# Channel mixing over token groups of 512, 512, 512 and 256, with every large tile at a multiple of 128 bytes

## The chip, the cores and the metric

The kernel runs on one core of one Trainium2 chip. TensorE (PE) multiplies matrices, VectorE (DVE) and ScalarE (ACT) do elementwise work and can read PSUM, GpSimd (POOL) does elementwise work in SBUF and issues some DMAs, SyncE (SP) issues most DMAs. The metric is the device time of the whole program in microseconds. Three timed runs of the kernel before gave 1157.68, 1158.13 and 1159.16 us; the median is 1158.13 us.

## The reference

Four batches of 448 tokens, 768 channels (12 heads of 64). Three stages follow each other:

```python
scores = scale * np.matmul(q, k.transpose(0, 1, 3, 2)) - np.log(S)
x = np.matmul(1.0 / (1.0 + np.exp(-scores)), v)      # stage 1, then heads side by side

h = x.transpose(0, 2, 1) @ U @ V                     # stage 2
u = x + h.transpose(0, 2, 1)
x = u + np.maximum(u @ w_ch1, 0.0) @ w_ch2           # channel mixing: 768 -> 3072 -> 768

theta = x @ w_theta                                  # stage 3
y = einsum(w_tok_r, x * cos(theta)) + einsum(w_tok_i, x * sin(theta))
u = x + y
out = u + np.maximum(u @ w_ch, 0.0)
```

The channel mixing does not couple tokens: it can be cut over the 4 x 448 = 1792 tokens at any place. The inputs `moe_w_ch1` and the others arrive as 64-bit floats and are turned into 32-bit ones inside the kernel.

## The kernel before

The running value `X` lies in SBUF as [128 channels of a block, 6 blocks, 1792 tokens], float32. To keep float32 accuracy with the one-pass matmul type fp32r, every operand is split into a high part and a low part (`uh`/`ul`, `gh`/`gl`, and two halves of each weight tile `w`), and each product is three matmuls: high x high, high x low, low x high.

The channel mixing is a loop over 12 blocks `i` of 256 hidden channels, and inside it over `b`, the four batches of 448 tokens. `ch1(i, b)` (lines 696 to 713) makes the hidden block: 2 x 6 x 3 = 36 matmuls of 128x128 weights against 448 moving columns into the PSUM tile `g`; then ACT takes the rectified value rounded to fp32r (`gh`, L709), and DVE the rest (`gl`, L710). `ch2(i, b)` (lines 715 to 729) multiplies back: 36 matmuls into three PSUM tiles `y` (two of them exist), and after each of them DVE adds the tile to `X` (L728). PE's order is `ch1` of a block, then `ch2` of the block before: 12 x 4 x 72 = 3456 matmuls in all, lines L702 to L704 and L724 to L726.

The order is written by hand (`manual_schedule`). Conversions of the next weights are jobs of a few steps, `size` on ACT, `bits`, `top`, `word` on DVE, then the split on ACT and POOL. The table `units` puts the steps at places `tick(i, b, t)`: t = 0 before `ch1`, t = 1 before `ch2`, t = 2 to 4 after its three additions. Each engine runs its own instructions in that order.

In the first block of all, `i` = 0, some of stage 2 is still going on. `split_u(b)` makes `uh` on ACT (L109) and `ul` on POOL (L112) or DVE (L118) from `X`. `U2(3)` (L495, L499, tile `hl`) adds the low-rank term of batch 3 to `X`; it runs between the pieces of `ch2(0, 0)`, and the splits of batch 2 stand behind it in the same hook, those of batch 3 one block later.

SBUF places: pools pad each tile to 32 bytes. `bias_s` and `half_pi` take 32 bytes each before `X`, so that in the built program `X` starts at byte 16576, 64 past a multiple of 128; with `warm` behind it, every other large tile starts 96 past one. All strides inside these tiles (1792, 3072, 512 bytes) are multiples of 128, so that every moving operand of an fp32r matmul starts 96 past a multiple of 128.

Of the kernel before, what the change touches and what calls it, by code (L numbers as in the profile page):

```python
# [19 lines left out]
def f(t):  # L20
    return t.bitcast(F32)
# [3 lines left out]
def tile_kernel(  # L25
# [20 lines left out]
    P = 128  # L46
# [40 lines left out]

    bias_s = cpool.tile([P, 1], F32, name="bias_s")
    half_pi = cpool.tile([P, 1], F32, name="half_pi")
    X = cpool.tile([P, NK, NT], F32, name="X")  # L90

    ctx.enter_context(tc.manual_schedule())
# [208 lines left out]
    ap2, ap2_st = pool("ap2")  # L301
    ident = ap2.tile([P, P], F32, name="ident")
    ps_a, ps_a_st = pool("ps_a", "left", PSUM)
# [268 lines left out]

    nc.vector.memset(bias_s, NEG_LOG_S)
    nc.vector.memset(half_pi, math.pi / 2)
    warm = cpool.tile([P, 1], F32, name="warm")
    load_qk(0)
# [22 lines left out]

    def split_u(b, p, d0, d1, *los):  # L600
        if d0 == 0:
            uh_t[b] = p.tile([P, NK, S], F32R, name=f"uh{b}")
            ul_t[b] = p.tile([P, NK, S], F32R, name=f"ul{b}")
# [88 lines left out]

    def ch1(i, b, js=range(FB)):
        if js[0] == 0:
            g_t[i, b] = ps_g.tile([P, FB, 512], F32, tag="g", name=f"g_{i}_{b}", bufs=2)
        ps = g_t[i, b]
        for j in js:
            wh, wl = w1_t[i, j][:, 0], w1_t[i, j][:, 1]
            for kk in range(NK):
                o = ps[:, j, :S]  # L700
                sl = slice(kk * P, (kk + 1) * P)
                nc.tensor.matmul(o, wh[:, sl], uh_t[b][:, kk, :], start=kk == 0, stop=False)  # L702
                nc.tensor.matmul(o, wh[:, sl], ul_t[b][:, kk, :], start=False, stop=False)  # L703
                nc.tensor.matmul(o, wl[:, sl], uh_t[b][:, kk, :], start=False, stop=kk == NK - 1)  # L704
        if js[-1] != FB - 1:
            return
        h = gpool.tile([P, FB, S], F32R, tag="gh", name=f"gh_{i}_{b}", bufs=2)
        l = gpool.tile([P, FB, S], F32R, tag="gl", name=f"gl_{i}_{b}", bufs=2)
# [6 lines left out]
    def ch2(i, b, after):  # L715
        gh, gl = g_t.pop((i, b))
        for e2 in range(NK // 2):
            ps = ps_y.tile([P, 2, 512], F32, tag="y", name=f"y_{i}_{b}_{e2}", bufs=2)
            for e in range(2):
                o = ps[:, e, :S]  # L720
# [20 lines left out]
    split_u(1, u[1][0], 0, NK, lo_pool, lo_dve)  # L741
    ch1(0, 0)
    ch1(0, 1, (0,))
# [3 lines left out]
    hi_act(vll, f(vl[:, (B - 1) % 2]))  # L747
    ch1(0, 1, (1,))
    ap_st.close()
    ps_a_st.close()  # L750

    u23, u23_st = pool("u23")
    ps_y, ps_y_st = pool("ps_y", "left", PSUM)
    def turn_x(b, d, t):
        nc.vector.transpose(out=t, in_=X[:, d, b * S:(b + 1) * S])
        nc.gpsimd.dma_start(out=x_d[d * P:(d + 1) * P, b * S:(b + 1) * S], in_=t)

    def hook(i, b):
# [361 lines left out]
```

## Time and profile before

| | |
|---|---|
| median of three runs | 1158.13 us |
| span of the profiled execution, first to last instruction | 1155.6 us |
| median less that span | 2.5 us |
| PE busy | 1144.3 us, 99% |
| DVE, ACT, POOL busy | 58%, 31%, 18% |
| channel mixing, first to last matmul | 162.9 to 869.8 us |

The profile records the start of each matmul. Its end is modelled, and a recorded duration (366 ns) is longer than the distance to the next start, since matmuls are pipelined; so a busy PE says only that work is queued, and the distance between starts says how fast it goes. PEld is the load of the 128x128 weights for the next matmul, which lies beside the matmul that runs.

### The profile page before, as it was taken

The numbers are of one execution on the slowest core, as the hardware profiler recorded it, in microseconds if no ns is written. First come the engines' busy times: TensorE is split into PE (matmuls) and PEld (weight loads), VectorE is DVE, ScalarE is ACT, GpSimd is POOL, SyncE is SP. The second block draws the span as 40 slices with busy tenths as digits, with TensorE's granted clock in tenths as the row PEclk, the third lists the DMA queues.
The fourth block names the chain that finished last, engine by engine and source line by source line (L and its number), as shares of the span: only waits on it lengthen the run. The fifth ranks groups of instructions, "written<-read, shape, count | busy, mean of one in ns | idle before, by whom it ended". The sixth has DMA issues, their size and how long they took to land.

```text
span 1155.6 us, 15709 instructions
## 1 busy us (share of the span) xinstructions
PE 1144.3 (99%) x6336; PEld 994.2 (86%) x6336; DVE 667.5 (58%) x831; ACT 358.0 (31%) x465; POOL 205.5 (18%) x172
## 2 busy tenths in 40 slices
PE   8999999999999999999999999999999999999998
PEld 5444468999999999999999999999999899999997
DVE  4787873445555555566566656656466643832443
ACT  6777863121212222222222222222014432730110
POOL 4120013210211111111221222111122321420000
PEclk9999999999999999999999999999999999999999
DMA  9898820113232423242414142413248410320444
GB/s 148 163 170 174 161 73 1 56 55 98 67 107 74 123 54 120 66 130 58 148 58 154 65 146 70 144 68 120 73 145 264 68 28 14 73 118 1 64 63 66
DMA packets 222568, 111.20 MB, mean 96 GB/s; under 512 B 188800, under 2 KB 212224, under 8 KB 222368
## 3 DMA queue, kind: packets, MB, share of 16 engines
q1 hardware_dynamic: 193856, 92.60, 31.6%
q0 software_dynamic: 4160, 14.21, 4.1%
q10 hardware_dynamic: 24480, 3.39, 2.0%
q8 instruction: 50, 0.82, 0.3%
q14 instruction: 22, 0.18, 0.1%
HBM read 86.51 MB, written 23.66 MB: 95 GB/s over the span
## 4 chain that ended last, share of the span: by engine, by line
PE 92%; DVE 3%; DMA 2%; ACT 1%; issue 1%; SPq 1%; ACTq 0%; DVEq 0%
PE g L702 10%; PE y L724 10%; PE y L725 10%; PE g L704 10%; PE g L703 10%; PE y L726 10%; PE av L439 4%; PE sc L413 3%; PE y L961 3%; PE y L959 3%; PE y L960 3%; PE wc L1084 2%; PE wc L1082 2%; PE wc L1083 2%; PE th L851 2%; PE th L847 2%
## 5 line engine op out<-in xcount | busy, mean ns | idle before, releaser
L728 DVE TENSOR_TENSOR X<-y,X 128x896 f32<-128x896 f32 x144 | 157.0, 1090 | 105.9 <-PE y L726 104.3
L702 PE MATMUL g<-uh,w 128*128 128x448 f32 x576 | 210.7, 366 | 0.0
L724 PE MATMUL y<-gh,w 128*128 128x448 f32 x576 | 210.6, 366 | 0.0
L704 PE MATMUL g<-uh,w 128*128 128x448 f32 x576 | 210.4, 365 | 0.0
L725 PE MATMUL y<-gl,w 128*128 128x448 f32 x576 | 210.4, 365 | 0.0
L726 PE MATMUL y<-gh,w 128*128 128x448 f32 x576 | 210.4, 365 | 0.0
L703 PE MATMUL g<-ul,w 128*128 128x448 f32 x576 | 210.4, 365 | 0.0
L709 ACT ACTIVATE gh<-g 128x896 fp32r<-128x896 f32 x48 | 44.1, 919 | 377.6 <-PE g L704 377.6
L710 DVE SCALAR_TENSOR_TENSOR gl<-g,gh 128x896 fp32r<-128x896 f32 x48 | 52.4, 1092 | 179.5 <-ACT gh L709 179.5
L112 POOL TENSOR_TENSOR w<-ca_w,w 128x768 fp32r<-128x768 f32 x42 | 77.9, 1854 | 423.2 <-ACT w L109 423.2
L702 PEld LDWEIGHTS g<-uh,w 128*128 128x128 f32 x576 | 108.2, 188 | 9.8 <-ACT uh L109 0.7
L724 PEld LDWEIGHTS y<-gh,w 128*128 128x128 f32 x576 | 108.2, 188 | 9.1 <-issue 0.6
L704 PEld LDWEIGHTS g<-uh,w 128*128 128x128 f32 x576 | 108.2, 188 | 8.6
L726 PEld LDWEIGHTS y<-gh,w 128*128 128x128 f32 x576 | 108.2, 188 | 8.5
L725 PEld LDWEIGHTS y<-gl,w 128*128 128x128 f32 x576 | 108.2, 188 | 8.5
L703 PEld LDWEIGHTS g<-ul,w 128*128 128x128 f32 x576 | 108.2, 188 | 8.5
L390 ACT ACTIVATE A<-sc,bias_s 128x896 f32<-128x896 f32 x72 | 69.9, 1006 | 7.5 <-PE sc L413 7.1
L156 DVE SCALAR_TENSOR_TENSOR ca_w<-ca_w,ws_w 128x768 uint32<-128x768 uint32 x48 | 60.0, 1251 | 3.8
L439 PE MATMUL av<-A,v 128*64 128x448 f32 x288 | 62.1, 552 | 0.0
L961 PE MATMUL y<-tok,zl 128*128 128x448 f32 x168 | 61.5, 366 | 0.3 <-DVE zl L118 0.3
L959 PE MATMUL y<-tok,zh 128*128 128x448 f32 x168 | 61.6, 367 | 0.2 <-ACT zh L109 0.2
L960 PE MATMUL y<-tok,zh 128*128 128x448 f32 x168 | 61.4, 366 | 0.0
(145 smaller groups left out, 1629.0 us busy)
## 6 DMA issues: line engine op xcount, KB each, us to landing
ws_w<-in_moe_w_ch_dram SPq DMA_DIRECT2D x40, 768.0 KB, 4.5
ws_w<-in_moe_w_ch_dram POOLq DMA_DIRECT2D x8, 768.0 KB, 5.5
x_d<-stg POOLq DMA_DIRECT2D x24, 224.0 KB, 2.5
k<-in_k_dram SPq DMA_DIRECT2D x90, 56.0 KB, 3.7
xn<-x_d SPq DMA_DIRECT2D x52, 96.0 KB, 3.3
q<-in_q_dram SPq DMA_DIRECT2D x89, 56.0 KB, 3.2
ws_th<-in_moe_w_theta_dram SPq DMA_DIRECT2D x6, 768.0 KB, 4.3
th_d<-sp_th SPq DMA_DIRECT2D x6, 768.0 KB, 4.0
```

What stands on the lines that cost most here:

```text
L112: nc.gpsimd.tensor_sub(o, a, b)
L439: nc.tensor.matmul(ps[h * D:(h + 1) * D, :S], v_t[p // 2][:, 2 * (p % 2) + h, c, :], A_t[p, c][:, h, :], start=c == 0 and p % 2 == 0, stop ...
L702: nc.tensor.matmul(o, wh[:, sl], uh_t[b][:, kk, :], start=kk == 0, stop=False)
L703: nc.tensor.matmul(o, wh[:, sl], ul_t[b][:, kk, :], start=False, stop=False)
L704: nc.tensor.matmul(o, wl[:, sl], uh_t[b][:, kk, :], start=False, stop=kk == NK - 1)
L724: nc.tensor.matmul(o, wh[:, sl], gh[:, j, :], start=j == 0, stop=False)
L725: nc.tensor.matmul(o, wh[:, sl], gl[:, j, :], start=False, stop=False)
L726: nc.tensor.matmul(o, wl[:, sl], gh[:, j, :], start=False, stop=j == FB - 1)
L728: nc.vector.tensor_add(x, ps[:, :, :S], x)
L959: nc.tensor.matmul(o, zh[:, sl], tok_h[:, i, :], start=first and n == 0, stop=False)
L960: nc.tensor.matmul(o, zh[:, sl], tok_l[:, i, :], start=False, stop=False)
L961: nc.tensor.matmul(o, zl[:, sl], tok_h[:, i, :], start=False, stop=last and n == len(slots) - 1)
```

## The change

The loop over batches in the channel mixing becomes a loop over `GRP`, four groups of 512, 512, 512 and 256 tokens. The number of blocks, of matmuls and of elementwise instructions stays; a matmul has 512 or 256 moving columns in place of 448. Tiles of `uh`, `ul`, `gh`, `gl`, `stg` get the new widths, and the pool of `uh`/`ul` for groups 2 and 3 becomes two pools. The small tiles go elsewhere or are 128 bytes wide, one tile of 96 bytes is put on the right side, and the scratch for software DMA descriptors is 8192 bytes per partition in place of 16384. In the built program every tile above 1 KB, `X` among them, now starts at a multiple of 128 bytes; this holds for the tiles of stages 1 and 3 too, whose widths stay. `gl` (the rectified low part) is emitted behind the first addition of the `ch2` that follows, in place of before it.

```diff
+    GB = 512
+    GRP = [(c, min(c + GB, NT)) for c in range(0, NT, GB)]
+    NG = len(GRP)
...
-    bias_s = cpool.tile([P, 1], F32, name="bias_s")
-    half_pi = cpool.tile([P, 1], F32, name="half_pi")
     X = cpool.tile([P, NK, NT], F32, name="X")
+
+    edge = ctx.enter_context(tc.tile_pool(name="edge", bufs=1, side="right"))
+    edge.tile([P, 24], F32, name="edge")
...
-    ident = ap2.tile([P, P], F32, name="ident")
+    ident = X[:, 0, :P]
+    bias_s, warm = (ap1.tile([P, R], F32, name=name)[:, :1] for name in ("bias_s", "warm"))
...
-    def split_u(b, p, d0, d1, *los):
+    def split_u(g, p, d0, d1, *los):
+        c0, c1 = GRP[g]
...
-            x = X[:, d, b * S:(b + 1) * S]
-            hi_act(uh_t[b][:, d], x)
-            los[d % len(los)](ul_t[b][:, d], x, uh_t[b][:, d])
+            x = X[:, d, c0:c1]
+            hi_act(uh_t[g][:, d], x)
+            los[d % len(los)](ul_t[g][:, d], x, uh_t[g][:, d])
...
-                o = ps[:, j, :S]
+                o = ps[:, j]
                 sl = slice(kk * P, (kk + 1) * P)
-                nc.tensor.matmul(o, wh[:, sl], uh_t[b][:, kk, :], start=kk == 0, stop=False)
+                nc.tensor.matmul(o, wh[:, sl], uh_t[g][:, kk, :], start=kk == 0, stop=False)
...
-        nc.scalar.activation(h, ps[:, :, :S], AF.Relu)
-        nc.vector.scalar_tensor_tensor(
-            out=l, in0=ps[:, :, :S], scalar=0.0, in1=f(h), op0=ALU.max, op1=ALU.subtract
-        )
-        g_t[i, b] = (h, l)
+        nc.scalar.activation(h, ps, AF.Relu)
+        g_t[i, g] = (h, l)
+
+        def low():
+            nc.vector.scalar_tensor_tensor(out=l, in0=ps, scalar=0.0, in1=f(h), op0=ALU.max, op1=ALU.subtract)
+        return low
...
-            x = X[:, 2 * e2:2 * e2 + 2, b * S:(b + 1) * S]
-            nc.vector.tensor_add(x, ps[:, :, :S], x)
+            x = X[:, 2 * e2:2 * e2 + 2, c0:c1]
+            nc.vector.tensor_add(x, ps, x)
+            if e2 == 0 and low is not None:
+                low()
             after(e2)
...
             if i == 0 and b in (1, 2):
-                split_u(b + 1, u23, 2 * e2, 2 * e2 + 2, lo_pool)
+                split_u(b + 1, u[b + 1][0], 2 * e2, 2 * e2 + 2, lo_pool)
...
-        for b in range(B):
+        for b in range(NG):
             tick(i, b, 0)
+            low = None
             if (i, b) not in ((0, 0), (0, 1)):
-                ch1(i, b)
+                low = ch1(i, b)
...
-    nc = _bacc.Bacc("TRN2", target_bir_lowering=False, num_devices=1)
+    nc = _bacc.Bacc("TRN2", target_bir_lowering=False, num_devices=1, dynamic_dma_scratch_size=8192)
```

DVE's rows in the iterations (0, 2) to (1, 0). The names are tiles with their block or group numbers: `gl` the low part, `y` the product back, `ws_w` and `ca_w` a weight in conversion. Before:

```order
L710 SCALAR_TENSOR_TENSOR gl_2_2406<-g_2_2368,gh_2_2405 128x896
L728 TENSOR_TENSOR X<-y_1_0_2409,X 128x2x448
L728 TENSOR_TENSOR X<-y_1_1_2429,X 128x2x448
L728 TENSOR_TENSOR X<-y_1_2_2447,X 128x2x448
L146 TENSOR_SCALAR ws_w_1_1_1742<-ws_w_1_1_1742 128x768
L150 SCALAR_TENSOR_TENSOR ws_w_1_1_1742<-ca_w_1_1_2467,ws_w_1_1_1742 128x768
L156 SCALAR_TENSOR_TENSOR ca_w_1_1_2467<-ca_w_1_1_2467,ws_w_1_1_1742 128x768
L710 SCALAR_TENSOR_TENSOR gl_3_2510<-g_3_2472,gh_3_2509 128x896
L728 TENSOR_TENSOR X<-y_2_0_2516,X 128x2x448
```

The same stretch of the changed kernel:

```order
L735 TENSOR_TENSOR X<-y_1_0_2412,X 128x2x512
L718 SCALAR_TENSOR_TENSOR gl_2_2410<-g_2_2372,gh_2_2409 128x1024
L735 TENSOR_TENSOR X<-y_1_1_2433,X 128x2x512
L735 TENSOR_TENSOR X<-y_1_2_2451,X 128x2x512
L150 TENSOR_SCALAR ws_w_1_1_1743<-ws_w_1_1_1743 128x768
L154 SCALAR_TENSOR_TENSOR ws_w_1_1_1743<-ca_w_1_1_2471,ws_w_1_1_1743 128x768
L160 SCALAR_TENSOR_TENSOR ca_w_1_1_2471<-ca_w_1_1_2471,ws_w_1_1_1743 128x768
L735 TENSOR_TENSOR X<-y_2_0_2519,X 128x2x512
L718 SCALAR_TENSOR_TENSOR gl_3_2514<-g_3_2476,gh_3_2513 128x2x256
```

`gl` of a block has moved from before the first addition to behind it, and the widths are 1024 and 2 x 256 in place of 896.

PE's rows at the end of `ch2(0, 0)`, where the last piece of `U2(3)` (`hl`) stands ahead of `ch1(0, 2)` (`g_2`). Before:

```order
L726 MATMUL y_0_2_2340<-gh_0_2173,w_0_1_1704 128x448
L495 MATMUL hl_2354<-vhl,pc_2253 128x448 x2
L499 MATMUL hl_2354<-vll,pc_2253 128x448 x2
L702 MATMUL g_2_2368<-uh_2310,w_0_0_1026 128x448
L703 MATMUL g_2_2368<-ul_2311,w_0_0_1026 128x448
```

The same place of the changed kernel:

```order
L733 MATMUL y_0_2_2341<-gh_0_2174,w_0_1_1705 128x512
L500 MATMUL hl_2355<-vhl,pc_2254 128x448 x2
L504 MATMUL hl_2355<-vll,pc_2254 128x448 x2
L707 MATMUL g_2_2372<-uh_2311,w_0_0_1027 128x512
L708 MATMUL g_2_2372<-ul_2312,w_0_0_1027 128x512
```

Nothing has moved here, but group 2 is tokens 1024 to 1535 and holds 192 tokens of batch 3 (from token 1344); its splits `uh`, `ul` now need the result of `hl`, pair of channel blocks by pair.

## Rows read from the trace of the kernel before

**Rows 1.** The page: span, engines' busy time, granted clock in 40 slices.
```profile
span 1155.6 us, 15709 instructions
...
PE 1144.3 (99%) x6336; PEld 994.2 (86%) x6336; DVE 667.5 (58%) x831; ACT 358.0 (31%) x465; POOL 205.5 (18%) x172
...
PEclk9999999999999999999999999999999999999999
```

**Rows 2.** Waits: who waited for whom, us in total, times, longest.
```profile
PE warm L596 <- POOL ident masks.py:199: 3.4, 1, 3.4
PE sc L413 <- DVE kl L118: 0.5, 1, 0.5
...
DVE gl L710 <- ACT gh L709: 179.5, 48, 7.3
```

**Rows 3.** Stretch of channel mixing: us, busy and (x) by engine, clock, DMA.
```profile
191.20:869.60 678.40, 678.40 (x3349) 628.82 (x3348) 391.89 (x410) 141.43 (x176) 120.50 (x79) 1.00 0.29 94
```

**Rows 4.** Timeline of PE, ends of channel mixing: start, us, engine, line.
```profile
191.17 0.47 PE L702 MATMUL g<-uh,w 128*128 128x448 f32 x1
...
869.80 0.34 PE L847 MATMUL th<-th_r,xh 128*128 128x384 f32 x1
```

**Rows 5.** Timeline of PE in the projection, 12 matmuls apart, 384 columns.
```profile
1000.60 0.33 PE L847 MATMUL th<-th_r,xh 128*128 128x384 f32 x1
...
1002.68 0.33 PE L847 MATMUL th<-th_r,xh 128*128 128x384 f32 x1
```

**Rows 6.** Timeline of PE in the token mixing, 18 matmuls apart, 448 columns.
```profile
1011.08 0.37 PE L961 MATMUL y<-tok,zl 128*128 128x448 f32 x1
...
1014.80 0.36 PE L961 MATMUL y<-tok,zl 128*128 128x448 f32 x1
```

**Rows 7.** Plain float32 transposes on PE: timeline, then durations min/median/max.
```profile
1015.00 0.82 PE L874 MATMUL xn<-ident_r,X 128*128 128x128 f32 x6
...
L874 PE MATMUL xn<-ident_r,X x6: 270/272/273, 1015.0 to 1015.5; 128*128 128x128 f32 x6
```

**Rows 8.** Timeline of PEld and PE, scores after a pause.
```profile
92.57 0.19 PEld L413 LDWEIGHTS sc<-qh,kh 64*128 64x128 f32 x2 [0.70 <-issue]
92.68 0.19 PEld L413 LDWEIGHTS sc<-ql,kh 64*128 64x128 f32 x2
...
92.88 0.36 PE L413 MATMUL sc<-ql,kh 64*128 64x448 f32 x2
```

**Rows 9.** Timeline: the last matmul of a tile, and the instruction that waited for it.
```profile
402.66 0.36 PE L704 MATMUL g<-uh,w 128*128 128x448 f32 x1
...
403.06 0.92 ACT L709 ACTIVATE gh<-g 128x896 fp32r<-128x896 f32 x1 [10.06 <-PE g L704]
...
1149.82 0.36 PE L1084 MATMUL wcl<-uh,wc_r 128*128 128x448 f32 x1
1150.22 0.62 DVE L1049 SCALAR_TENSOR_TENSOR X<-wcl,X 128x448 f32<-128x448 f32 x1 [2.34 <-PE wcl L1084]
```

**Rows 10.** Groups of instructions by shape: busy us, mean ns, idle before.
```profile
L728 DVE TENSOR_TENSOR X<-y,X 128x896 f32<-128x896 f32 x144 | 157.0, 1090 | 105.9 <-PE y L726 104.3 <-POOL ul L112 1.3
L960 PE MATMUL y<-tok,zh 128*128 128x448 f32 x168 | 61.4, 366 | 0.0
L710 DVE SCALAR_TENSOR_TENSOR gl<-g,gh 128x896 fp32r<-128x896 f32 x48 | 52.4, 1092 | 179.5 <-ACT gh L709 179.5
L848 PE MATMUL th<-th_r,xh 128*128 128x384 f32 x168 | 56.1, 334 | 0.0
L1083 PE MATMUL wc<-ul,wc_r 128*128 128x448 f32 x132 | 48.2, 365 | 0.0
```

**Rows 11.** Timeline around 181 to 192 us: splits of batch 2, addition of `hl`.
```profile
181.34 2.91 ACT L109 ACTIVATE uh<-X 128x448 fp32r<-128x448 f32 x6
...
181.99 6.71 POOL L112 TENSOR_TENSOR ul<-X,uh 128x448 fp32r<-128x448 f32 x6 [12.95 <-ACT uh L109]
...
191.28 1.09 DVE L503 TENSOR_TENSOR X<-hl,X 128x896 f32<-128x896 f32 x1
```

More of the change, by code (lines that the diff above doesn't have):

```diff
@@ L573, in tile_kernel @@
     nc.vector.memset(bias_s, NEG_LOG_S)
-    nc.vector.memset(half_pi, math.pi / 2)
-    warm = cpool.tile([P, 1], F32, name="warm")
     load_qk(0)
@@ L598, in tile_kernel @@
     uh_t, ul_t, g_t = {}, {}, {}
-    def split_u(b, p, d0, d1, *los):
+    def split_u(g, p, d0, d1, *los):
+        c0, c1 = GRP[g]
         if d0 == 0:
-            uh_t[b] = p.tile([P, NK, S], F32R, name=f"uh{b}")
-            ul_t[b] = p.tile([P, NK, S], F32R, name=f"ul{b}")
+            uh_t[g] = p.tile([P, NK, c1 - c0], F32R, name=f"uh{g}")
+            ul_t[g] = p.tile([P, NK, c1 - c0], F32R, name=f"ul{g}")
         for d in range(d0, d1):
-            x = X[:, d, b * S:(b + 1) * S]
-            hi_act(uh_t[b][:, d], x)
-            los[d % len(los)](ul_t[b][:, d], x, uh_t[b][:, d])
+            x = X[:, d, c0:c1]
+            hi_act(uh_t[g][:, d], x)
+            los[d % len(los)](ul_t[g][:, d], x, uh_t[g][:, d])
     warm_up(26)
@@ L691, in tile_kernel, with ch1 @@
     ps_g, ps_g_st = pool("ps_g", "right", PSUM)
-    def ch1(i, b, js=range(FB)):
+    def ch1(i, g, js=range(FB)):
+        w = GRP[g][1] - GRP[g][0]
         if js[0] == 0:
-            g_t[i, b] = ps_g.tile([P, FB, 512], F32, tag="g", name=f"g_{i}_{b}", bufs=2)
-        ps = g_t[i, b]
+            g_t[i, g] = ps_g.tile([P, FB, GB], F32, tag="g", name=f"g_{i}_{g}", bufs=2)
+        ps = g_t[i, g][:, :, :w]
         for j in js:
@@ L699, in ch1, with ch2 @@
             for kk in range(NK):
-                o = ps[:, j, :S]
+                o = ps[:, j]
                 sl = slice(kk * P, (kk + 1) * P)
-                nc.tensor.matmul(o, wh[:, sl], uh_t[b][:, kk, :], start=kk == 0, stop=False)
-                nc.tensor.matmul(o, wh[:, sl], ul_t[b][:, kk, :], start=False, stop=False)
-                nc.tensor.matmul(o, wl[:, sl], uh_t[b][:, kk, :], start=False, stop=kk == NK - 1)
+                nc.tensor.matmul(o, wh[:, sl], uh_t[g][:, kk, :], start=kk == 0, stop=False)
+                nc.tensor.matmul(o, wh[:, sl], ul_t[g][:, kk, :], start=False, stop=False)
+                nc.tensor.matmul(o, wl[:, sl], uh_t[g][:, kk, :], start=False, stop=kk == NK - 1)
         if js[-1] != FB - 1:
             return
-        h = gpool.tile([P, FB, S], F32R, tag="gh", name=f"gh_{i}_{b}", bufs=2)
-        l = gpool.tile([P, FB, S], F32R, tag="gl", name=f"gl_{i}_{b}", bufs=2)
-        nc.scalar.activation(h, ps[:, :, :S], AF.Relu)
-        nc.vector.scalar_tensor_tensor(
-            out=l, in0=ps[:, :, :S], scalar=0.0, in1=f(h), op0=ALU.max, op1=ALU.subtract
-        )
-        g_t[i, b] = (h, l)
-    def ch2(i, b, after):
-        gh, gl = g_t.pop((i, b))
+        h = gpool.tile([P, FB, GB], F32R, tag="gh", name=f"gh_{i}_{g}", bufs=2)[:, :, :w]
+        l = gpool.tile([P, FB, GB], F32R, tag="gl", name=f"gl_{i}_{g}", bufs=2)[:, :, :w]
+        nc.scalar.activation(h, ps, AF.Relu)
[3 more added lines that the diff above has]
+        return low
+    def ch2(i, g, after, low):
+        c0, c1 = GRP[g]
+        gh, gl = g_t.pop((i, g))
         for e2 in range(NK // 2):
-            ps = ps_y.tile([P, 2, 512], F32, tag="y", name=f"y_{i}_{b}_{e2}", bufs=2)
+            ps = ps_y.tile([P, 2, GB], F32, tag="y", name=f"y_{i}_{g}_{e2}", bufs=2)[:, :, :c1 - c0]
             for e in range(2):
-                o = ps[:, e, :S]
+                o = ps[:, e]
                 sl = slice((2 * e2 + e) * P, (2 * e2 + e + 1) * P)
@@ L741, in tile_kernel @@
     split_u(1, u[1][0], 0, NK, lo_pool, lo_dve)
-    ch1(0, 0)
+    ch1(0, 0)()
     ch1(0, 1, (0,))
@@ L747, in tile_kernel, with turn_x @@
     hi_act(vll, f(vl[:, (B - 1) % 2]))
-    ch1(0, 1, (1,))
+    ch1(0, 1, (1,))()
     ap_st.close()
     ps_a_st.close()
-    u23, u23_st = pool("u23")
+    u.append(pool("u2"))
     ps_y, ps_y_st = pool("ps_y", "left", PSUM)
-    def turn_x(b, d, t):
-        nc.vector.transpose(out=t, in_=X[:, d, b * S:(b + 1) * S])
-        nc.gpsimd.dma_start(out=x_d[d * P:(d + 1) * P, b * S:(b + 1) * S], in_=t)
+    def turn_x(g, d, t):
+        c0, c1 = GRP[g]
+        nc.vector.transpose(out=t[:, :c1 - c0], in_=X[:, d, c0:c1])
+        nc.gpsimd.dma_start(out=x_d[d * P:(d + 1) * P, c0:c1], in_=t[:, :c1 - c0])
     def hook(i, b):
         def after(e2):
-            if i == L and 0 < b < B:
+            if i == L and 0 < b < NG:
                 for d in (2 * e2, 2 * e2 + 1):
-                    turn_x(b - 1, d, late["stg"].tile([P, S], F32, tag="stg", name=f"stg_{b}_{d}", bufs=4))
+                    turn_x(b - 1, d, late["stg"].tile([P, GB], F32, tag="stg", name=f"stg_{b}_{d}", bufs=4))
             if (i, b) == (0, 1):
@@ L803, in tile_kernel @@
                 th_t[0] = load_kept("th0", "w1")
-            if i == L and b == B - 1:
+            if i == L and b == NG - 1:
                 th_t[2] = load_kept("th2", "w1")
@@ L810, in tile_kernel @@
             if prev is not None:
-                ch2(*prev, hook(i, b))
+                ch2(*prev, hook(i, b), low)
             prev = (i, b)
@@ L814, in tile_kernel @@
                 uv_st.close()
+                u.append(pool("u3"))
                 late["sp"], sp_st = pool("sp")
-    ch2(*prev, hook(NB - 1, B))
+    ch2(*prev, hook(NB - 1, NG), None)
     th_t[4] = load_kept("th4", "w2")
@@ L821, in tile_kernel @@
     stg_st.close()
-    u23_st.close()
+    u[3][1].close()
+    u[2][1].close()
     gpool_st.close()
@@ L834, in tile_kernel @@
     ctx.enter_context(st)
+    half_pi = zp.tile([P, R], F32, name="half_pi")[:, :1]
+    nc.vector.memset(half_pi, math.pi / 2)
     T_t, z_t, pj_t = {}, {}, {}
@@ L990, in tile_kernel @@
     for d in range(NK):
-        t = zp.tile([P, 2, HN], F32, tag="zh", name=f"stg_{B}_{d}", bufs=12).rearrange("p a n -> p (a n)")[:, :S]
-        turn_x(B - 1, d, t)
+        t = zp.tile([P, 2, HN], F32, tag="zh", name=f"stg_{NG}_{d}", bufs=12).rearrange("p a n -> p (a n)")
+        turn_x(NG - 1, d, t)
     project(0, th_t, "th", 0, 4)
```

## The prediction

> **What bounds the kernel now.** I read the page first: PE is busy for 1144.3 of 1155.6 us and its clock is granted in nine tenths or more in every slice, and in full, 2.4 GHz, over the stage in question; DVE is busy for 58% [rows 1, 3]. The list of waits then says whether PE waits for anyone. It hardly does: its longest wait is 3.4 us for the identity at the very start, and no other matmul waits more than half a microsecond in all. DVE's 179.5 us before `gl` are a wait of an engine that is not the bound [rows 2]. So only two things can change the time: how far apart the starts of PE's matmuls are, and a new wait of PE.
>
> The changed stage is pure PE: in the stretch from 191.2 to 869.6 us PE is busy for all of 678.4 us, DVE for 391.9 [rows 3]. From the first matmul of `ch1(0, 2)` to the first after the stage are 869.80 - 191.17 = 678.63 us; 108 of the 3456 matmuls lie before, so these are 3348, and one start follows the other by 678.63 / 3348 = 202.7 ns [rows 4]. 448 columns at 2.4 GHz would be 186.7 ns. 16.0 ns per matmul, or 3456 x 16.0 = 55 us, is thus not columns, and the change is decided by what these 16 ns are.
>
> Four other rows bear on it. With 384 columns 12 matmuls take 2.08 us, 173.3 ns each: 160.0 of columns and 13.3 more, 32 cycles [rows 5]. With 448 columns in the token mixing 18 take 3.72 us, 206.7 each: 20.0 more [rows 6]. The same width thus runs at two rates, depending on how the stream of matmuls has settled; the narrower 384 is tighter. Plain float32 transposes, which take two cycles per column, are (0.82 - 0.27) / 5 = 0.11 us apart, 106.7 of columns and some 3 more [rows 7]: changing weights alone costs nearly nothing when the columns are read at half the pace. And the load of the next weights is not what costs: the last matmul of the kernel, with no load behind it, releases DVE 0.40 us after its start, and one with a load beside it releases ACT after the same 0.40 us [rows 9].
>
> **The change part by part.**
>
> *Widths.* The number of matmuls and of columns stays: 864 matmuls in each of the four groups, 864 x 4 x 448 = 864 x (3 x 512 + 256). If the extra per matmul stayed at 16.0, nothing would change: 864 x (3 x 229.3 + 122.7) = 700.4 us against 3456 x 202.7 = 700.5. It matters only if the extra depends on width or place. The trace has no matmul of 512 or 256 columns, so I bound it. From below by the transposes, some 2 to 3 ns [rows 7]; from above by the worse rate of 448, 20.0 [rows 6]. The nearest row is 384 columns, whose width is a whole number of 128-column pieces, as 512 and 256 are, while 448 is three and a half: 13.3 ns [rows 5]. I take it: 512 columns at 226.7, 256 at 120.0. The stage is then 864 x (3 x 226.7 + 120.0) = 691.3 us, 9.2 us less.
>
> A group of 256 must still hide its weight load. After a pause the second load starts 0.11 us after the first, and the second matmul 0.31 us after the first load, that is one load of about 0.11 and one matmul of 0.20 [rows 8]. A load thus holds its place for some 110 ns, less than 120: I cost it at nothing, with 10 ns of cover.
>
> *Places.* Every large tile moves from 96 past a multiple of 128 bytes to a multiple. No row here has an operand in another place, so the trace can't show what that does. Nothing is the upper bound; the lower one is that the whole extra goes, down to some 2 ns (a rival below). [...] I take nothing for the sum.
>
> *The low part.* On DVE `gl` goes behind the first addition of `ch2`. Before, it waited at the head of DVE's queue for `gh`, and the first addition and the conversion steps stood behind it. Who needs it? The `ch2` of its own block, which is one `ch1` and more away, over 9 us. In the groups the order counts: where a `ch2` of 256 columns follows a `ch1` of 512, a tile `y` is done after 12 x 0.120 = 1.4 us, and the third needs the first one's addition by 2.9 us. With `gl` (1.09 us for 896 elements, so some 1.25 for 1024 [rows 10]) ahead and `gh` ahead of that, the addition would come too late; with `gl` behind it, the addition ends near 2.4 us. So the new order hides itself: nothing gained against before, nothing lost. DVE's work per round of 58.4 us is 33.7 us as before, scaled from [rows 3], and the elements don't change.
>
> *A new wait at the start.* Before, the splits of batch 2 ran from 181.34 us on ACT and until 181.99 + 6.71 = 188.70 on POOL, all done before `ch1(0, 2)` began at 191.17 [rows 4, 11]. Now group 2 holds tokens of batch 3, and its last two channel blocks wait for the last addition of `hl`, from 191.28 to 192.37 [rows 11]. Behind it ACT makes two of 512 (2.91 / 6 x 512 / 448 = 0.55 us each), POOL two of 6.71 / 6 x 512 / 448 = 1.28 each: the last `ul` is ready near 192.37 + 0.55 + 2 x 1.28 = 195.5. PE reaches it after 5 channel blocks of three matmuls and one more, 16 x 0.227 = 3.6 us behind 191.3, at 194.9. It waits 0.6 us; ACT's and POOL's starts add some tenths. I take 1.0 us, once; queued behind it on PE is the whole stage. Bounds: 0 and 3 us, the three additions' whole delay.
>
> *The rest.* The first pieces of group 0 and 1 need batches 1 and 2, whose low-rank terms are added before the stage begins. `half_pi`, `ident` and the bias cost the same instructions at another place. Half the descriptor scratch could hold back a software DMA of POOL; POOL is 18% busy [rows 1], and nothing of its queue ends a wait of PE [rows 2]: nothing.
>
> *The sum.* 1155.6 - 9.2 + 1.0 = 1147.4 us of span. The median of the runs lies 2.5 us above the span of the profiled execution: 1149.9, say 1150 us.
>
> **The rivals.**
>
> *The place was the cost (faster by far).* The 13.3 ns of the 384 columns are 32 cycles, just what 128 bytes of a float32 row take at one column per cycle: a row of 12 such pieces that starts 96 bytes into one touches 13. Float32 at half the pace hides it [rows 7]. If a matmul pays for pieces touched, an operand at a multiple of 128 pays none: extra of about 2 ns, so 512 at 215.3 and 256 at the weight load's 110. The stage is 864 x (3 x 215.3 + 110) = 653.1 us, 47.4 less. It would also hold in the other stages: 504 matmuls of 384 columns save 11.3 ns each, 5.7 us; 504 and 432 of 448 columns 14 ns each, 7.1 and 6.0 us [rows 10]; the scores some 1.5. With the wait, 1158.1 - 67.7 + 1.0 = 1091 us. For it speaks how well the number fits; against it, that a fixed turn-around of 32 cycles, hidden by float32's slack too, fits as well. [...]
>
> *A fixed extra (no change).* 16.0 ns whatever the width: -0.1 + 1.0, 1159 us. For it: the extra of 384 and 448 differs by less than 3 ns.
>
> *The stream settles badly (slower).* The rate of 20.0 ns extra is in the trace for the same instructions [rows 6]. If all groups settle there, 864 x (3 x 233.3 + 126.7) = 714.2 us, 13.7 more: 1158.1 + 13.7 + 1.0 = 1173 us. It decides from a mean extra of 16.0 on. Against it: 448 columns ran at 202.7 over 3348 matmuls and left the bad rate at the first pause. A kin of it, the weight load of a 256-column group showing, costs 0.86 us per ns; with 512 at 226.7 the gain is gone when 256 takes over 130.7.
>
> **How the numbers follow.** My forecast has a chance of 0.34, its own range 1146 to 1154. The place as the cost has 0.32 (partial forms between 1100 and 1140 in it), the fixed extra 0.14, the bad rate and its kin 0.20. A change of up to 0.2%, 2.3 us, can't be told from none. Faster is 0.34 + 0.32 = 0.66, same 0.14, slower 0.20. The range leaves out the slower cases and the far edge of the second: 1080 to 1163 us.
>
> **What would show it.** The distance of starts in the stage: 226.7 and 120.0 ns bear out the forecast, 229.3 and 122.7 the fixed extra, about 215 and 110 the place; then the 384 columns of the projection, whose width stays, must also fall from 173.3 to about 162, and that alone tells place from width. A new wait of `g` on POOL `ul` near 195 us, under 3 us, shows the start. PE waits for DVE in `y` would prove the order of `gl` wrong.

## The result, and the profile after

The changed kernel takes 1148.47 us (median of 4 runs, 1148.02 to 1148.97), the kernel before 1158.56 us (4 runs, 1157.68 to 1159.16). The ratio is 0.9916, 95% interval 0.9904 to 0.9928: faster, and within 2 us of the forecast of 1150.

The page after has the same form as [rows 1]. PE is still the bound, with a mean granted clock of 0.999 over the span.

```profile
span 1147.1 us, 15707 instructions
...
PE 1135.5 (99%) x6336; PEld 934.7 (81%) x6336; DVE 667.2 (58%) x831; ACT 358.4 (31%) x465; POOL 204.0 (18%) x172
...
PEclk9999999999999999999999999999999999999999
```

To see where the 8.5 us of span went I split both executions at the first matmul of the channel mixing and at the first one after it, and let the view of windows sum each stretch (columns as in [rows 3]). Before, then after:

```profile
162.93:869.80 706.87, 706.87 (x3582) 653.06 (x3581) 406.90 (x427) 152.02 (x197) 131.53 (x88) 1.00 0.29 91
```

```profile
160.69:860.50 699.81, 699.14 (x3583) 593.99 (x3582) 408.47 (x427) 152.66 (x198) 129.98 (x88) 1.00 0.29 93
```

The stage is 7.06 us shorter (forecast 9.2 - 1.0 = 8.2). It starts 2.24 us earlier, which the forecast had at nothing. What follows it, 1155.6 - 869.80 = 285.8 us before, is 1147.1 - 860.50 = 286.6, 0.8 longer. The sum is 8.5 us.

The medians lie further apart, 10.1 us. Every timed run takes 1.7 to 1.9 us more than its span, so the profiled executions stand for about 1157.4 us before, a short one of its kernel (median 1158.56), and 1148.9 us after, a long one (1148.47). The start that a single profile shows may therefore be off by a microsecond or two.

The starts of PE's matmuls after, in its timeline (start, duration, line): 12 apart with 512 columns, 12 apart with 256, and 12 apart in the projection, whose 384 columns stay (compare [rows 5]):

```profile
299.84 0.39 PE L731 MATMUL y<-gh,w 128*128 128x512 f32 x1
...
302.56 0.39 PE L731 MATMUL y<-gh,w 128*128 128x512 f32 x1
```

```profile
288.05 0.28 PE L731 MATMUL y<-gh,w 128*128 128x256 f32 x1
...
289.49 0.28 PE L731 MATMUL y<-gh,w 128*128 128x256 f32 x1
```

```profile
991.58 0.33 PE L862 MATMUL th<-th_r,xh 128*128 128x384 f32 x1
...
993.66 0.33 PE L862 MATMUL th<-th_r,xh 128*128 128x384 f32 x1
```

That is 2.72 / 12 = 226.7 ns, 1.44 / 12 = 120.0 ns and 2.08 / 12 = 173.3 ns. A step of 128 columns is worth 53.3 ns, from 120.0 to 173.3 as from there to 226.7: 0.417 ns per column, or 2.4 columns per ns, as the forecast counted. Below, "beyond the columns" is beyond that time. The first two are the forecast's numbers; the third has not moved, so the rival in which the place was the cost (about 162 ns) is out.

PE's waits in the whole execution, as in [rows 2], now hold two of the channel mixing:

```profile
PE g L708 <- POOL ul L116: 0.4, 2, 0.3
...
PE y L731 <- DVE X L735: 0.2, 1, 0.2
```

The timeline shows the first of them where it was expected, in the first block of group 2:

```profile
191.80 1.08 DVE L508 TENSOR_TENSOR X<-hl,X 128x896 f32<-128x896 f32 x1
...
192.92 1.15 ACT L113 ACTIVATE uh<-X 128x512 fp32r<-128x512 f32 x2 [2.79 <-DVE X L508]
...
193.62 2.52 POOL L116 TENSOR_TENSOR ul<-X,uh 128x512 fp32r<-128x512 f32 x2 [1.41 <-ACT uh L113]
...
194.40 0.39 PE L707 MATMUL g<-uh,w 128*128 128x512 f32 x1
194.96 0.50 PE L708 MATMUL g<-ul,w 128*128 128x512 f32 x1 [0.18 <-POOL ul L116]
...
195.54 0.40 PE L707 MATMUL g<-uh,w 128*128 128x512 f32 x1
...
196.20 0.51 PE L708 MATMUL g<-ul,w 128*128 128x512 f32 x1 [0.26 <-POOL ul L116]
```

The list counts 0.4 us of wait, but the distance of starts is the price: 0.56 and 0.66 us in place of 0.227, and 0.34 in place of 0.227 for the start that follows each (196.20 to 196.54), 0.77 + 0.23 = 1.0 us in all. So these two stops cost PE 1.0 us where the view names 0.4.

### The profile page after: what moved, and what is told of

The parts are those of the page before. It is cut to its first block, busy times and chain, and to the rows that moved or that the text cites. A ratio compares the mean times of both kernels' runs of the same rounds, so it can differ in the third digit from the quotient of the medians.

```text
span 1147.1 us, 15707 instructions
## 1 busy us (share of the span) xinstructions
PE 1135.5 (99%) x6336; PEld 934.7 (81%) x6336; DVE 667.2 (58%) x831; ACT 358.4 (31%) x465; POOL 204.0 (18%) x172
## 4 chain that ended last, share of the span: by engine, by line
PE 78%; DVE 3%; ACT 1%; issue 0%; POOL 0%; POOLq 0%; DVEq 0%; ACTq 0%
PE y L731 10%; PE y L732 10%; PE y L733 10%; PE g L708 10%; PE g L709 9%; PE g L707 9%; PE y L976 3%; PE y L975 3%; PE y L974 3%; PE wc L1098 2%; PE wc L1099 2%; PE wc L1097 2%; PE th L866 2%; PE th L863 2%; PE th L862 2%; DVE xl L122 1%
## 5 line engine op out<-in xcount | busy, mean ns | idle before, releaser
L735 DVE TENSOR_TENSOR X<-y,X 128x1024 f32<-128x1024 f32 (+1 forms) x144 | 156.6, 1088 | 262.6 <-PE y L733 251.2
L708 PE MATMUL g<-ul,w 128*128 128x512 f32 (+1 forms) x576 | 209.2, 363 | 0.4 <-POOL ul L116 0.4
L731 PE MATMUL y<-gh,w 128*128 128x512 f32 (+1 forms) x576 | 209.3, 363 | 0.2 <-DVE X L735 0.2
L707 PE MATMUL g<-uh,w 128*128 128x512 f32 (+1 forms) x576 | 209.3, 363 | 0.0
L732 PE MATMUL y<-gl,w 128*128 128x512 f32 (+1 forms) x576 | 208.9, 363 | 0.0
L709 PE MATMUL g<-uh,w 128*128 128x512 f32 (+1 forms) x576 | 208.8, 363 | 0.0
L733 PE MATMUL y<-gh,w 128*128 128x512 f32 (+1 forms) x576 | 208.8, 362 | 0.0
L714 ACT ACTIVATE gh<-g 128x1024 fp32r<-128x1024 f32 (+1 forms) x48 | 44.2, 921 | 376.2 <-PE g L709 376.2
L732 PEld LDWEIGHTS y<-gl,w 128*128 128x128 f32 x576 | 108.7, 189 | 16.7
L116 POOL TENSOR_TENSOR zl<-t,zh 128x768 fp32r<-128x768 f32 x21 | 39.4, 1894 | 102.8 <-ACT zh L113 77.2
```

The costliest lines, as they stand in the source:

```text
L116: nc.gpsimd.tensor_sub(o, a, b)
L707: nc.tensor.matmul(o, wh[:, sl], uh_t[g][:, kk, :], start=kk == 0, stop=False)
L708: nc.tensor.matmul(o, wh[:, sl], ul_t[g][:, kk, :], start=False, stop=False)
L709: nc.tensor.matmul(o, wl[:, sl], uh_t[g][:, kk, :], start=False, stop=kk == NK - 1)
L735: nc.vector.tensor_add(x, ps, x)
```

## The experiments

Two theories of the 9.2 us were open (width or place), three parts of the change could be undone one at a time, and the 2.2 us at the start had no theory. "Start" below is the first matmul of the channel mixing, "stage" the time from there to the first matmul after it. The kernel before was timed beside each set: 1158.73 us for the first four kernels, 1159.41 for the second four, 1158.71 for the last.

### Places alone, on the kernel before

```diff
+    warm = cpool.tile([P, 1], F32, name="warm")
+    cpool.tile([P, 8], F32, name="pad")
     X = cpool.tile([P, NK, NT], F32, name="X")
...
+    edge = ctx.enter_context(tc.tile_pool(name="edge", bufs=1, side="right"))
+    edge.tile([P, 24], F32, name="edge")
...
-    warm = cpool.tile([P, 1], F32, name="warm")
```

> The kernel before with its four batches of 448 tokens, every large tile moved to a multiple of 128 bytes, nothing else. Fixed extra by width (our theory): the place pays nothing, starts in channel mixing stay within 202.6 to 206.7 ns, the 384 columns of the projection at 173.3; time 1158.6 us within 2, or up to 1164 if the 448-column streams settle at the 204.0 ns that the 448-column matmuls of the changed kernel show (3456 + 936 matmuls x 1.35 ns = 5.9 us more). Rival, the place was the cost: 448 at about 189, 384 at about 162, 1091 to 1100 us. Open besides: in the changed kernel channel mixing began 2.2 us earlier (160.7 against 162.9 us). If the places did that, it begins at 160.7 here; if the transfers of the first stage scatter, anywhere from 160 to 163.

1158.02 us, ratio 0.9997 (0.9988 to 1.0005). The stage did not get faster:

```profile
159.76:868.91 709.15, 709.15 (x3582) 652.98 (x3581) 406.96 (x427) 152.40 (x197) 131.61 (x88) 1.00 0.29 91
```

709.15 us against 706.87. But it started at 159.76, 3.2 us earlier than before; the matmuls gave that back, 2.3 us in the stage, where the 448 columns settled at a mean of 203.4 ns from `ch1(0, 2)` on, not 202.7, and 0.8 us behind it. There the 384 columns of the projection, expected at 173.3 ns, lie 5.28 / 30 = 176.0 ns apart (30 matmuls):

```profile
979.71 0.34 PE L851 MATMUL th<-th_r,xh 128*128 128x384 f32 x1
...
984.99 0.34 PE L851 MATMUL th<-th_r,xh 128*128 128x384 f32 x1
```

So these places made neither of these two kinds of matmuls faster, and yet the stage starts 3.2 us earlier, so they do something to stage 1. The changed kernel has the same kinds of tiles at multiples of 128 and keeps 173.3; why this kernel does not is open.

### Groups alone, at the old places

```diff
+    cpool.tile([P, 16], F32, name="pad0")
     X = cpool.tile([P, NK, NT], F32, name="X")
-    edge = ctx.enter_context(tc.tile_pool(name="edge", bufs=1, side="right"))
-    edge.tile([P, 24], F32, name="edge")
+    cpool.tile([P, 8], F32, name="pad1")
```

> The changed kernel with its groups of 512, 512, 512 and 256, its tiles put back to 96 past a multiple of 128 bytes as before. Our theory: starts of 226.7 and 120.0 ns as in the changed kernel, the 448 columns of the later stages back from 204.0 to 202.6 (936 x 1.35 = 1.3 us less): 1147 us if the early start of channel mixing isn't due to the places, 1149.5 if it is. Rival, that the places are what makes 512 and 256 tight: starts of about 229.3 and 122.7, 1157 to 1159 us.

1152.96 us, ratio 0.9955 (0.9943 to 0.9966).

```profile
165.42:865.21 699.79, 699.10 (x3582) 593.93 (x3581) 408.49 (x427) 152.92 (x198) 130.21 (x88) 1.00 0.29 93
```

The stage is that of the changed kernel, 699.79 against 699.81 us: its gain belongs to the groups and needs no place. The 4.5 us by which this kernel's median is longer lie ahead of the stage, which starts at 165.42 us (4.7 of the 5.1 us between the two spans). One number of the first 155 us goes with the place, the mean busy share of the DMA engines (next to last column of the windows), at the same rate of 161 GB/s (last column). Before, after, and this kernel:

```profile
0.00:155.00 155.00, 150.15 (x1266) 74.75 (x1268) 114.77 (x205) 117.29 (x153) 26.80 (x53) 1.00 0.88 161
```

```profile
0.00:155.00 155.00, 150.37 (x1280) 75.67 (x1280) 115.06 (x205) 119.05 (x154) 26.82 (x53) 1.00 0.77 161
```

```profile
0.00:155.00 155.00, 147.68 (x1252) 72.64 (x1252) 111.72 (x200) 116.39 (x150) 26.91 (x53) 1.00 0.90 161
```

The waits of the first 165 us name whom it hurts: DVE, which transposes `q` and `k` as they land. Before, after, then here:

```profile
DVE qT L360 <- DMA q<-in_q_dram: 10.0, 6, 2.5
DVE kT L372 <- DMA k<-in_k_dram: 6.9, 2, 6.1
```

```profile
DVE kT L377 <- DMA k<-in_k_dram: 4.7, 1, 4.7
...
DVE qT L365 <- DMA q<-in_q_dram: 3.2, 3, 1.4
```

```profile
DVE qT L364 <- DMA q<-in_q_dram: 18.1, 12, 4.9
...
DVE kT L376 <- DMA k<-in_k_dram: 8.8, 3, 5.9
```

### Only the tiles of q and k at multiples of 128

The kernel just shown, with 32 bytes put into the pool that holds `q`, `k` and their transposed and split forms; all other large tiles stay 96 past (`X` 64).

```diff
+    ap2.tile([P, 8], F32, name="pad2")
```

> The kernel with the new groups but the large tiles back at 96 past a multiple of 128 bytes, and in it the tiles of one pool alone (q and k as loaded, with their transposed and split forms) again at multiples of 128. Theory (the place counts for the transfers of q and k, which DVE waits for in stage 1): the channel mixing starts at 160 to 161.5 us in place of 165.4, DMA is busy for about 0.77 in place of 0.90 of the first 155 us, and the time is 1148 to 1149 us. Rival (another tile's place, or nothing of the transfers): start 165.4 us, 1153 us.

1149.04 us (1148.79 to 1149.09), ratio 0.9916 (0.9903 to 0.9930). The start is 160.46 us and the share is back at 0.76:

```profile
0.00:155.00 155.00, 150.75 (x1280) 75.74 (x1282) 115.43 (x205) 119.20 (x155) 26.82 (x53) 1.00 0.76 161
```

So the place works through this one pool. Of its tiles only `q` and `k` are written by transfers, and the view of DMA issues says that these very transfers got shorter (KB each, median us from issue to landing). The groups at old places, then this kernel:

```profile
k<-in_k_dram SPq DMA_DIRECT2D x90, 56.0 KB, 3.8
...
q<-in_q_dram SPq DMA_DIRECT2D x89, 56.0 KB, 3.4
```

```profile
k<-in_k_dram SPq DMA_DIRECT2D x90, 56.0 KB, 3.1
...
q<-in_q_dram SPq DMA_DIRECT2D x89, 56.0 KB, 2.8
```

`v` lands sooner too (6.2 us, then 4.5), though its tiles did not move, so part of this may be that less stands in the queues. All of it points at the landing place of `q` and `k` as the cause, and not at a tile that the engines make from them: the same bytes keep the DMA engines busy for less, 0.76 against 0.90. It is argued from these rows; the pool's tiles were not moved one by one.

### The smaller scratch alone

```diff
-    nc = _bacc.Bacc("TRN2", target_bir_lowering=False, num_devices=1)
+    nc = _bacc.Bacc("TRN2", target_bir_lowering=False, num_devices=1, dynamic_dma_scratch_size=8192)
```

> The kernel before with the scratch for software DMA descriptors halved to 8192 bytes, everything else as it was, places too. Theory (the scratch counts for nothing, as forecast): channel mixing starts at 162.9 us and the time is 1158.6 us. Rival (the smaller scratch is what made the kernel with new groups and old places start its channel mixing at 165.4 us, against 162.9 before): start near 165.4 us, 1161 us.

1158.09 us, ratio 0.9990 (0.9981 to 0.9999), start 163.79. The scratch costs nothing, as forecast. Why the groups at old places started at 165.4 and the kernel before at 162.9 is not settled; the executions of that kernel spread from 1151.71 to 1153.95 us, and the profiled one was the longest, 1.0 us above the median, while the profiled execution before, at about 1157.4 us, lies 1.3 below the median of 1158.73 beside it. If the scatter of a kernel lies ahead of the stage, which no run shows, it makes up 2.3 of these 2.5 us.

### The low part ahead of the first addition again

```diff
-                low = ch1(i, b)
+                ch1(i, b)()
```

> The changed kernel with the low part made before the first addition again, as in the kernel before. Our theory: where the product back of a 256-token group follows the hidden block of a 512-token group, gh ends 1.25 us after that hidden block, the low part 1.25 later, and the first addition (0.7) at 3.2; the third piece should start at 2.9. PE waits about 0.4 to 0.5 us in each of 11 rounds, on y for DVE's X: 4 to 6 us more, 1153 us. Rival: two tiles y are enough and DVE's order costs PE nothing, 1148.5 us.

1152.72 us, ratio 0.9953 (0.9941 to 0.9965): 4.25 us of the gain are gone. A `ch2` of 256 columns behind a `ch1` of 512 shows it in the timeline:

```profile
288.88 1.23 DVE L718 SCALAR_TENSOR_TENSOR gl<-g,gh 128x1024 fp32r<-128x1024 f32 x1 [5.40 <-ACT gh L714]
...
290.02 1.36 DVE L735 TENSOR_TENSOR X<-y,X 128x512 f32<-128x512 f32 x2
...
290.38 0.28 PE L733 MATMUL y<-gh,w 128*128 128x256 f32 x1
290.76 0.39 PE L731 MATMUL y<-gh,w 128*128 128x256 f32 x1
290.98 0.28 PE L732 MATMUL y<-gl,w 128*128 128x256 f32 x1
```

DVE makes the low part until 290.11, so the addition that frees the tile `y` ends near 290.7, and the third tile's first matmul starts 0.38 us after the one before it and the next 0.22 after that, each in place of 0.12. These 0.36 us come in 11 of the rounds, 4.0 us, which is what the stage has grown by (703.79 us).

### The low part behind the addition, on the kernel before

The same move alone, with 448 columns and old places:

```diff
+        def low():
+            nc.vector.scalar_tensor_tensor(
+                out=l, in0=ps[:, :, :S], scalar=0.0, in1=f(h), op0=ALU.max, op1=ALU.subtract
+            )
+        return low
...
             nc.vector.tensor_add(x, ps[:, :, :S], x)
+            if e2 == 0 and low is not None:
+                low()
```

> The kernel before, 448 columns and old places, with the low part alone moved behind the first addition of the product that follows. Theory (the order gains nothing where all groups are of one width, since the low part is due a block later): the stage stays 706.9 us long, 1158.6 us. Rival (DVE's head-of-queue wait of 179.5 us before the low part cost PE something): shorter by 0.5 us or more within the stage.

1158.59 us, ratio 0.9999 (0.9990 to 1.0008), stage 707.04 us against 706.87. DVE's 179.5 us of waiting ahead of the low part [rows 2] cost PE nothing in this stage. The move is worth 4.25 us with the narrow groups of the changed kernel and nothing without them here.

### Other widths: 512, 480, 416, 384

```diff
-    GRP = [(c, min(c + GB, NT)) for c in range(0, NT, GB)]
+    GRP = [(0, 512), (512, 992), (992, 1408), (1408, 1792)]
```

> The changed kernel with groups of 512, 480, 416 and 384 tokens: four widths in one look. Starts if only whole pieces of 128 columns run at 13.3 ns extra: 226.7, 216 to 220, 189.3 to 193.3, 173.3. If any multiple of 32 columns does: 226.7, 213.3, 186.7, 173.3. If the extra grows with the width (12 columns in 13 cycles): 231.1, 216.7, 187.8, 173.3; the 512 and 256 of the changed kernel speak against that.

1152.92 us in one run. In both products the starts settle 226.7 ns apart with 512 columns and 173.3 with 384, tight, that is 13.3 ns beyond the columns. The other two widths vary from matmul to matmul (210 to 223 and 182 to 195 ns); in blocks without a wait their means, from the ninth start on, are 218.5 ns in `ch1` and 216.7 in `ch2` with 480 columns, 187.9 and 188.2 with 416: 16.7 to 18.5 and 14.6 to 14.9 ns beyond the columns. Of these four, the two widths of whole 128 columns run tight, the other two don't.

In `ch1` the distance of an operand's rows changes with the width too: 2048 and 1536 bytes are whole multiples of 512, 1920 and 1664 are not, nor are the 1792 of before. In `ch2` it does not: `gh` and `gl` are cut from rows of 512 floats, 2048 bytes, whatever the width. There 12 matmuls of 480 columns take 2.60 us, 216.7 ns each, where 213.3 would be tight:

```profile
260.00 0.38 PE L733 MATMUL y<-gh,w 128*128 128x480 f32 x1
...
262.60 0.38 PE L733 MATMUL y<-gh,w 128*128 128x480 f32 x1
```

So the width counts by itself: rows of the same 2048 bytes hold 512 columns at 13.3 ns beyond the columns and 480 at 16.7. Whether the row distance counts too is what the next three kernels ask.

### Longer rows, and operands off their places

The changed kernel, columns as in it, with rows of the moving operands 128 bytes longer, and the operand 0, 4 or 16 bytes into its row (the edit for 4; for `ul`, `gh` and `gl` likewise):

```diff
-            uh_t[g] = p.tile([P, NK, c1 - c0], F32R, name=f"uh{g}")
+            uh_t[g] = p.tile([P, NK, c1 - c0 + 32], F32R, name=f"uh{g}")[:, :, 1:c1 - c0 + 1]
```

> The changed kernel with the four kinds of moving operands of the channel mixing (high and low parts of X and of the rectified block) starting one float, 4 bytes, past a multiple of 128 in rows 128 bytes longer. Theory (place is nothing to a matmul): starts stay 226.7 and 120.0 ns apart. Rival (a matmul pays for each stretch of 16 or 128 bytes that it touches): one more stretch, so some 4 to 14 ns more per matmul, 14 to 48 us in all.

> The changed kernel with the rows of the four kinds of moving operands 128 bytes longer (544 floats in place of 512, 288 in place of 256), each operand still starting at a multiple of 128. Control of the shift by one float, which has this longer row too and runs 512 columns 236.6 ns apart. Theory (the shift of 4 bytes costs): 226.7 and 120.0 ns, 1148 to 1149 us. Rival (the longer row, another distance between operands, costs): 236 ns, 1173 us.

> The same longer rows with the operands starting four floats, 16 bytes, past a multiple of 128. Theory A (a matmul pays where an operand does not start at a multiple of 16 bytes): 226.7 and 120.0 ns, 1148 to 1149 us, as at 96 past. Theory B (it pays for anything but a multiple of 32): 236 and 120.7 ns, 1173 us, as for a shift of 4 bytes.

One run each: 1173.08 us at 4 bytes, 1160.83 at 0, 1156.28 at 16. Their stages, in this order:

```profile
159.96:884.65 724.69, 724.42 (x3583) 597.92 (x3581) 409.37 (x427) 152.96 (x198) 127.69 (x88) 1.00 0.28 90
```

```profile
160.65:872.38 711.73, 711.10 (x3582) 592.49 (x3581) 409.26 (x427) 152.65 (x198) 130.51 (x88) 1.00 0.29 91
```

```profile
160.39:867.81 707.42, 706.79 (x3582) 592.12 (x3581) 409.15 (x427) 152.75 (x198) 130.62 (x88) 1.00 0.29 92
```

Neither theory nor rival was right for the control. The longer row alone costs 11.9 us: 512 columns lie 231.95 ns apart on the mean in place of 227.0, in a spread from 224 to 236, while 256 columns are not slower (119.0). A start 4 bytes into the row adds 4.7 ns more (236.6), one 16 bytes into it nothing (230.7; that stage is even 4.3 us shorter than the control's). So a matmul of 512 columns does not run tight because of its width alone: with the rows of its operands 2048 bytes apart it does (226.7 ns), with rows 2176 bytes apart it does not (231.95). That whole multiples of 512 bytes are what counts was not shown. Rows of 2048 bytes alone are not enough either, as 480 and 416 columns in `ch2` show (216.7 and 188.2 ns). 448 columns in rows of 2048 bytes were not run.

### Groups in the order 512, 256, 512, 512

```diff
-    GRP = [(c, min(c + GB, NT)) for c in range(0, NT, GB)]
+    GRP = [(0, 512), (512, 768), (768, 1280), (1280, 1792)]
...
-                    turn_x(b - 1, d, late["stg"].tile([P, GB], F32, tag="stg", name=f"stg_{b}_{d}", bufs=4))
+                    turn_x(b - 1, d, late["stg"].tile([P, GB], F32, tag="stg", name=f"stg_{b}_{d}", bufs=3))
```

> The changed kernel with the groups in the order 512, 256, 512, 512. Group 2 is then tokens 768 to 1279 and holds none of batch 3, so its splits need nothing of the last low-rank addition. Theory (the wait at the start costs about 1.0 us): no wait of the tile g on the low splits near 195 us, the rest unchanged, 1147.5 us, about 1 us less than the changed kernel's 1148.5. Rival (the wait is hidden or moves: group 3, made one group later, or the shorter second group exposes something else): the same 1148.5 us or more.

1151.71 us, ratio 0.9942 (0.9929 to 0.9955): 3.2 us worse than the changed kernel, a miss; the stage takes 702.78 us, 3.0 more. The wait is gone from group 2 and comes back larger in group 3 (waits of PE, then the timeline):

```profile
PE g L708 <- POOL ul L116: 2.4, 3, 1.0
```

```profile
198.12 9.27 POOL L116 TENSOR_TENSOR ul<-X,uh 128x512 fp32r<-128x512 f32 x6 [13.18 <-ACT uh L113]
```

The splits of group 3, six of 512 on POOL, stand behind ACT's `gh` of group 2, and the `ch2` that should cover them has 256 columns, 4.3 us, where they take 9.3. In the changed kernel the narrow group is the last, and its splits are half as long.

### The last two splits on DVE

```diff
-                split_u(b + 1, u[b + 1][0], 2 * e2, 2 * e2 + 2, lo_pool)
+                split_u(b + 1, u[b + 1][0], 2 * e2, 2 * e2 + 2, lo_dve if (b, e2) == (1, 2) else lo_pool)
```

> The changed kernel with the low splits of group 2's last two channel blocks made by DVE in place of POOL. Theory (the wait at the start is POOL's two splits of 1.28 us behind the last addition): DVE takes some 0.6 us each, the last is ready near 194.7 us, PE's wait in the first block of group 2 falls from about 1.0 us to under 0.3, and the time is 1147.6 us, 0.7 to 1.0 us below the changed kernel. Rival (the order that moved the wait to group 3 when the groups were reordered does so here too, or DVE's additions come late): 1148.5 us or more, with a new wait in the first 50 us of the channel mixing.

1147.56 us (1146.95 to 1148.03), ratio 0.9904 (0.9890 to 0.9917). No `g` waits for a split any more. DVE has both done at 192.90 + 1.30 = 194.20, and the matmul that needs the last starts at 194.63:

```profile
192.90 1.30 DVE L122 TENSOR_TENSOR ul<-X,uh 128x512 fp32r<-128x512 f32 x2 [0.70 <-ACT uh L113]
...
194.63 0.39 PE L708 MATMUL g<-ul,w 128*128 128x512 f32 x1
```

The stage is 698.76 us, 1.05 shorter than in the changed kernel: the wait's price, taken away. The interval of the ratio overlaps that of the changed kernel, so the trace shows this gain, and the times only point the same way. It is the best version seen.

## Why the prediction was right

*Widths: right to a tenth of a nanosecond, for half a reason.* 226.7 and 120.0 ns were forecast and found, and the groups give the same stage at either place. The step took 13.3 ns from 384 columns because that width is whole 128-column pieces. That counts in these runs: 480 and 416 columns do not run tight even in rows of 2048 bytes (16.7 and 14.9 ns beyond the columns). It is not all: 512 columns in rows of 2176 bytes cost 18.6 ns beyond the columns. The step did not ask about the rows; that the change puts 512 columns into rows of 2048 bytes was luck. Why the two matter stays open. The lower bound of 2 to 3 ns came from the transposes, 0.11 us for 128 columns [rows 7], about twice the 53.3 ns found here. That this is two cycles per column, and not for instance the load of some 0.11 us [rows 8], was an estimate that no run tested. No width of the channel mixing came near that bound: the lowest mean over a stage is 11.3 (256 columns, 16 bytes into longer rows, 118.0 ns).

*The stage came out 1.1 us longer than its sum.* The sum left out the edges between widths: the first five starts of 512 columns behind a group of 256 are 2 to 9 ns longer, and added up over the 23 such changes, less what the 24 changes the other way give back, this is 0.5 us. And the last `ch2`, of 256 columns, stands straight behind another `ch2`, so that its third tile waits for DVE (the wait of `y` in the list, 0.2 us); from start to start that is 0.51 and then 0.22 us in place of 0.12 each (858.46, 858.97, 859.19 us), 0.5 us lost.

*The weight load under 256 columns: right.* 256 columns take 120.0 ns, 13.3 beyond the columns, and 512 take 226.7, the same 13.3 beyond: no load shows in the narrow ones.

*Places: nothing, and this was the step that failed.* No row of the kernel before shows this term of the sum; in its place the runs showed two things. For a matmul it held in the changed kernel: 384 columns stay at 173.3 and the stage of the new groups takes 699.8 us at either place (on the kernel before the new places cost the 384 columns 2.7 ns). But the step asked only about the moving operands. The places of `q` and `k` as they land are moved too, and they carry a gain of 4.5 us in time (groups with and without the places). Against the kernel before, the profiles show a start that is 2.2 us earlier, with a short execution before and a long one after. DVE's waits for `q` and `k` stood in the trace of before, 10.0 and 6.9 us, and I gave them no price. The busy share of the DMA engines goes with the place, 0.75 to 0.78 against 0.88 to 0.90; how the place does it, no run shows. Of the start of a moving operand the runs with longer rows show that a shift of 4 bytes costs 4.7 ns per matmul of 512 columns (236.6 against 231.95) and one of 16 bytes nothing (230.7).

*The low part: right.* Undone, it costs 4.25 us through the third tile, as the step said; alone on the kernel before it is worth nothing (1158.59 against 1158.71 us). The sign that was to prove the step wrong, a wait of `y` for DVE, did appear once, 0.2 us at the last `ch2`; that block has no low part behind its first addition, so the order of `gl` is not its cause.

*The new wait: right in place, cause and size.* Forecast 1.0 us, from 194.9 to 195.5 with some tenths; found 1.0. The last `ul` was ready at 193.62 + 2.52 = 196.14, 0.6 us later than worked out, since the last addition of `hl` began 0.5 us later (191.80 against 191.28) and POOL 0.1 behind ACT's first split; PE was 0.4 us later too. Taken off POOL, it is gone and the stage is 1.05 us shorter.

*Scratch: right, nothing.*

*The sum.* That the span came out at 1147.1 us, forecast 1147.4, is partly luck: the sum left out a gain of 2.2 us at the start and losses of 1.1 + 0.8 us behind it, which cancel to within 0.3 us. The last term, 2.5 us from span to median, was mis-sized: it held 1.8 us, which every timed run has, and 0.7 us because the profiled execution before was short; after the change it is 1.4. The 0.8 us behind the stage are mostly the 448-column matmuls of the last stage, which settled at 203.9 ns here (1100.41 to 1104.08 us, 18 apart) and 202.8 before (1108.28 to 1111.93). Before, then after:

```profile
1108.28 0.36 PE L1083 MATMUL wc<-ul,wc_r 128*128 128x448 f32 x1
...
1111.93 0.36 PE L1083 MATMUL wc<-ul,wc_r 128*128 128x448 f32 x1
```

```profile
1100.41 0.37 PE L1098 MATMUL wc<-ul,wc_r 128*128 128x448 f32 x1
...
1104.08 0.37 PE L1098 MATMUL wc<-ul,wc_r 128*128 128x448 f32 x1
```

They do so at old places too where the groups are new (mean 204.0 ns), and not at new places with the old groups (202.7), so place isn't the cause; what a stream settles at remains open.

## What to carry to other kernels

When PE is the bound and waits for no one, measure the distance of starts per width, and look for the operand layout at which it is lowest, here 512 columns in rows 2048 bytes apart, 226.7 ns, against 231.95 in rows of 2176; a change of tile width can also be a change of row distance, so test the two apart. When tiles move in SBUF, ask for every transfer that lands in them, not only for the engine that reads them: the places of `q` and `k` were worth 3.9 us here (1152.96 to 1149.04). And with narrow groups look first at the order in the queues of the elementwise engines, which have less time to free a tile: the three pieces of a `ch2` take 4.3 us with 256 columns against 7.3 with 448 (36 starts of 120.0 and of 202.7 ns), and the low part ahead of the first addition cost 4.25 us.

## What the runs showed that I had not expected

- The same transfers, at 161 GB/s in the first 155 us, keep the DMA engines busy for 0.88 to 0.90 of it with their tiles 96 bytes past a multiple of 128, and for 0.75 to 0.78 at a multiple.
- 128 bytes more in the rows of the moving operands cost a stage of pure matmuls 11.9 us of 700, and a start 4 bytes into the row 13.0 us more. In rows of 2048 bytes 480 columns still lie 216.7 ns apart, 16.7 beyond the columns.
- A wait that the list gives as 0.4 us cost 1.0: the list counts from the modelled end of the matmul before, and each of the two restarts added 0.11 us to the start that followed.
